# Eight consecutive w2 rows per partition, and the last outputs behind earlier DMAs

## The chip, the cores and the metric

The kernel runs on one core of one Trainium2 chip. The core has a tensor engine (PE), a vector engine (DVE), a scalar engine (ACT), GpSimd (POOL in the profile) and a sync engine (SP), which share an on-chip memory of 128 partitions. Sixteen DMA engines move data between it and the device memory. In this kernel GpSimd and SP issue the DMAs. The metric is the time of one execution on the device, in microseconds; the median of several runs counts.

## The reference

Two layers run one after the other. The first is attention over 8 batches, 8 heads, 576 positions and a head size of 64. Four heads look back over a window of 32 positions, the other four over every fourth position in a window of 128. The second is a soft mixture of 8 experts with 4 slots each:

```python
x = attn_out.transpose(0, 2, 1, 3).reshape(4608, 512)
logits = x @ phi                        # 4608 x 32
d = softmax(logits, axis=0)             # over the rows
slot_input = (d.T @ x).reshape(8, 4, 512)
for e in range(8):
    h = np.maximum(slot_input[e] @ w1[e], 0.0)   # 4 x 1024
    slot_out[e] = h @ w2[e]                      # w2[e]: 1024 x 512
c = softmax(logits, axis=1)
out = c @ slot_out.reshape(32, 512)     # 4608 x 512
```

All inputs and the output are fp32. The slots need every row of x, so nothing of the output can start before the attention of all batches, the weights w1 and w2 of the experts, and the small products between them are done.

## The kernel before

The kernel casts every input to fp16 while it is loaded: only GpSimd's DMAs (the calls on `nc.gpsimd`) do this here, so all loads stand in GpSimd's order. A loop over the batches runs in three slots each (`slot0`, `slot1`, `slot2`), which lay out by hand in which order scores, exponentials, products with v, and the products for the mixture are issued, two batches deep. The loads of later batches and of the weights are issued from inside these slots (`weights`, lines 531 to 563): w1 in the first six batches and at the start of the seventh, w2 from the seventh on. Before a GpSimd load is issued, the load issued eight places before must have landed.

**w2.** Each expert's w2 has 1024 rows of 512 numbers. `load_w2` (line 217) brings them into a tile of 128 partitions, 8 rows each. In the kernel before, partition p holds rows 4p to 4p+3 in its first half and rows 512+4p to 512+4p+3 in its second, so a partition is filled from two runs of 8 KB in the device memory. There are three forms of load:

- whole experts (1 to 5): one DMA of all 128 partitions (line 219);
- expert 0: one DMA of partitions 0 to 95, and later four DMAs of 8 partitions each (`load_w2_eight`, line 523: partitions 96+j, 100+j, ... 124+j). Each of these four is followed by a tiny load of 8 x 8 numbers into `turn`, which nothing reads;
- experts 6 and 7: four DMAs each (line 227), by column half and by rows 0 to 3 or 4 to 7 of each partition. The first column halves of both come first.

**From slots to h.** After the batches, PE computes h for all 32 slots in two PSUM tiles of 512 columns, `hps[0]` and `hps[1]` (line 686). ACT and DVE take half the columns of each with a relu into `h_sb[fc]` (lines 696 and 697). Four PE transposes per tile (line 699) pick every fourth column, to match the rows that a partition of w2 holds; copies on DVE and ACT put the result into `hTm` (line 703).

**The output.** `slot_out` (line 718) multiplies `hTm` by w2, one column half at a time, and ACT copies the result to `so_sb`. Then `out` is made in pairs of 128-row blocks. Rows of the first pairs 0 to 7 are made in two column halves (`combine`), those of pairs 8 to 17 whole (`combine_full`). A pair is a product on PE, a scaling out of PSUM on ACT or DVE, and an output DMA. The order of the last ones is: whole pair 13, half pair 3, whole 14, half 4, whole 15, half 5, half 6, half 7, whole 16, whole 17. All go out by GpSimd in fp16, cast on the way, except whole pairs 16 and 17: these are written in fp32 and go out by SP.

**The buffers at the end.** Pairs 16 and 17 use two fp32 buffers that are used once before: `last0` by whole pair 15, and `last1` by half pair 5 (in fp16, in a part of the buffer). So the scaling of pair 16 has to wait until the output DMA of whole pair 15 has landed, and that of pair 17 until that of half pair 5 has.

The lines that matter:

```python
in_=moe_w2[e].rearrange("(h p l) n -> p h (l n)", h=2, l=4)[rows],          # line 221
nc.tensor.transpose(hT[fc][:, c, :], h_sb[fc].rearrange("p (k l) -> p l k", l=4)[:, c, :], ident)   # 699
if (half, pair) == (1, 5):                                                   # 764, takes "last1"
tag = "last1" if pair == NFIN // 2 - 1 else "last0"                          # 794, NFIN // 2 is 18
```

Of the kernel before, what the change touches and what calls it, by code (L numbers as in the profile page):

```python
# [9 lines left out]
FP32 = mybir.dt.float32  # L10
FP16 = mybir.dt.float16
U32 = mybir.dt.uint32
AF = mybir.ActivationFunctionType
# [11 lines left out]
DMODEL = H * D  # L25
# [3 lines left out]
FDIM = 1024  # L29
# [12 lines left out]
NFIN = N_ROWS // 128  # L42
UNITS = 7
MASKED = -60000.0
NH = DMODEL // 2
# [4 lines left out]
def kernel(  # L50
# [10 lines left out]
    nc = tc.nc  # L61
# [11 lines left out]
    ident = consts.tile([128, 128], FP16, name="ident")  # L73
# [14 lines left out]
    w2t = {e: w2a_pool.tile([128, 8, DMODEL], FP16, name=f"w2_{e}", tag=f"w2_{e}") for e in range(2)}  # L88
# [12 lines left out]
    for i in range(NV):  # L101
        slab = fix.tile([128, V_SLAB], FP16, name=f"v{i}", tag=f"v{i}")
        n = NT * 4 * VW
# [113 lines left out]
    def load_w2(e, half=None, rows=slice(0, 128)):  # L217
        if half is None:
            nc.gpsimd.dma_start(  # L219
                out=w2t[e].rearrange("p (h l) n -> p h (l n)", h=2)[rows],  # L220
                in_=moe_w2[e].rearrange("(h p l) n -> p h (l n)", h=2, l=4)[rows],
            )
            return
        src = moe_w2[e].rearrange("(h p l) n -> h p l n", h=2, l=4)
        c0 = NH * half
        for h in range(2):
            nc.gpsimd.dma_start(
                out=w2t[e][:, 4 * h : 4 * h + 4, c0 : c0 + NH], in_=src[h][:, :, c0 : c0 + NH]
            )


# [291 lines left out]
    def load_w2_eight(j):  # L523
        load_w2(0, rows=slice(96 + j, 128, 4))
        nc.gpsimd.dma_start(out=turn[0:8, 8 * j : 8 * j + 8], in_=moe_w2[0, 0:8, 0:8])
# [131 lines left out]
    h_pool = tc.alloc_tile_pool(name="hp", bufs=1)  # L657
    out_pool = tc.alloc_tile_pool(name="outp", bufs=1)
# [5 lines left out]
    for g in range(4):  # L664
# [8 lines left out]
        out=diag,  # L673
# [6 lines left out]
    hps = [psum_e.tile([128, 512], FP32, name=f"hps{fc}", tag=f"hps{fc}") for fc in range(2)]  # L680
    for fc in range(2):
        for g in range(2):
            for dc in range(4):
                for j in range(4):
                    e = 4 * g + j
# [4 lines left out]
                        start=(g == 0 and dc == 0),  # L690
                        stop=(g == 1 and dc == 3),
                    )
    h_sb = [h_pool.tile([128, 512], FP16, name=f"h_sb{fc}", tag=f"h_sb{fc}") for fc in range(2)]
    hT = [psum_e.tile([128, 4, 128], FP16, name=f"hT{fc}", tag=f"hT{fc}") for fc in range(2)]
    for fc in range(2):
        nc.scalar.activation(out=h_sb[fc][:, 0:256], in_=hps[fc][:, 0:256], func=AF.Relu)
        nc.vector.tensor_relu(out=h_sb[fc][:, 256:512], in_=hps[fc][:, 256:512])
        for c in range(4):
            nc.tensor.transpose(hT[fc][:, c, :], h_sb[fc].rearrange("p (k l) -> p l k", l=4)[:, c, :], ident)
        hT4 = hT[fc].rearrange("p c (j s) -> p c j s", j=4)  # L700
        for g in range(2):
            dst = hTm[2 * g + fc].rearrange("p c (j s) -> p c j s", j=4)[:, :, :, 16 * g : 16 * g + 16]
            (nc.vector.tensor_copy, nc.scalar.copy)[g](out=dst, in_=hT4[:, :, :, 16 * g : 16 * g + 16])
# [30 lines left out]
    def combine_one(half, blk):  # L734
        fp = psum_f.tile([128, NH], FP32, name=f"f{half}_one{blk}", tag="f")
        cols = slice(NH * half, NH * half + NH)
        r0 = 128 * blk
        nc.tensor.matmul(fp, ET[:, r0 : r0 + 128], so_sb[:, cols], start=True, stop=True)
        ot = out_pool.tile([128, NH], FP16, name=f"oo{half}_{blk}", tag=f"oo{half}_{blk}")
        if blk % 2 == 0:  # L740
            nc.scalar.activation(out=ot, in_=fp, func=AF.Copy, scale=rrow[:, blk : blk + 1])
        else:
            nc.vector.tensor_scalar(
                out=ot, in0=fp, scalar1=rrow[:, blk : blk + 1], scalar2=None, op0=ALU.mult
            )
        nc.gpsimd.dma_start(out=out[r0 : r0 + 128, cols], in_=ot)

    def combine(half, pair):
        if half == 0 and pair == 0:
            combine_one(half, 0)  # L750
            combine_one(half, 1)
            return
        fp = psum_f.tile([128, 2, NH], FP32, name=f"f{half}_{pair}", tag="f")
        r0 = 256 * pair
        for k in range(2):
            nc.tensor.matmul(
                fp[:, k, :],
                ET[:, r0 + 128 * k : r0 + 128 * k + 128],
                so_sb[:, NH * half : NH * half + NH],
                start=True,  # L760
                stop=True,
                skip_group_check=True,
            )
        if (half, pair) == (1, 5):
            ot = out_pool.tile([128, 2, DMODEL], FP32, name="last1_a", tag="last1")
            ot = ot[:, 0, 0:NH].bitcast(FP16).rearrange("p (k n) -> p k n", k=2)
        else:
            ot = out_pool.tile(
                [128, 2, NH], FP16, name=f"ot{half}_{pair}", tag=f"ot{half}", bufs=NSPLIT // 2 - half
            )  # L770
        if pair % 2 == 0:
            for k in range(2):
                blk = 2 * pair + k
                nc.scalar.activation(
                    out=ot[:, k, :], in_=fp[:, k, :], func=AF.Copy, scale=rrow[:, blk : blk + 1]
                )
        else:
            nc.vector.tensor_tensor(
                out=ot,
                in0=fp,  # L780
                in1=rrow[:, 2 * pair : 2 * pair + 2, None].broadcast_to([128, 2, NH]),
                op=ALU.mult,
            )
        nc.gpsimd.dma_start(
            out=out[r0 : r0 + 256, NH * half : NH * half + NH].rearrange("(k p) n -> p k n", k=2),
            in_=ot,
        )

    def combine_full(pair):
        r0 = 256 * pair  # L790
        if pair < NFIN // 2 - 3:
            ot = out_pool.tile([128, 2, DMODEL], FP16, name=f"of_{pair}", tag="of", bufs=6)
        else:
            tag = "last1" if pair == NFIN // 2 - 1 else "last0"
            ot = out_pool.tile([128, 2, DMODEL], FP32, name=f"ol_{pair}", tag=tag)
            if pair == NFIN // 2 - 3:
                ot = ot[:, 0, :].bitcast(FP16).rearrange("p (k n) -> p k n", k=2)
        for k in range(2):
            blk = 2 * pair + k
            fp = psum_f.tile([128, DMODEL], FP32, name=f"f_{blk}", tag="f")  # L800
            nc.tensor.matmul(fp, ET[:, 128 * blk : 128 * blk + 128], so_sb, start=True, stop=True)
            if k == 0:
                nc.scalar.activation(
                    out=ot[:, k, :], in_=fp, func=AF.Copy, scale=rrow[:, blk : blk + 1]
                )
            else:
                nc.vector.tensor_scalar(
                    out=ot[:, k, :],
                    in0=fp,
                    scalar1=rrow[:, blk : blk + 1],  # L810
                    scalar2=None,
                    op0=ALU.mult,
                )
        (nc.gpsimd if pair < NFIN // 2 - 2 else nc.sync).dma_start(
            out=out[r0 : r0 + 256, :].rearrange("(k p) n -> p k n", k=2), in_=ot
        )

    with tc.manual_schedule(engines=None):
        slot_out(0, ORDER[:6])
        slot_out(1, ORDER[:6])  # L820
        slot_out(0, HALVED)
        at = {5: 0}
        for pair in range(NSPLIT // 2):
            combine(0, pair)
            if pair in at:
                slot_out(1, (HALVED[at[pair]],))
        slot_out(1, HALVED[1:])
        for pair in range(NSPLIT // 2, NFIN // 2 - 2):
            combine_full(pair)
            if pair >= NFIN // 2 - NSPLIT // 2:  # L830
                combine(1, pair - (NFIN // 2 - NSPLIT // 2))
        for pair in range(2):
            combine(1, NSPLIT // 2 - 2 + pair)
        for pair in range(2):
            combine_full(NFIN // 2 - 2 + pair)
# [36 lines left out]
```

The softmax here doesn't subtract the row's maximum and nothing guards it: scores larger than these inputs give would overflow.

## Time and profile before

| | |
|---|---|
| median of four runs | 183.19 us (182.41 to 183.41) |
| the profiled execution | 183.05 us, its span 181.4 us |
| PE / DVE / ACT / POOL busy | 81% / 59% / 50% / 46% of the span |
| DMA | 40.75 MB by written size, mean 225 GB/s |
| read / written in device memory | 61.93 MB / 9.44 MB |
| w2, whole experts (5 DMAs) | 1024 KB each, 19.4 us from issue to landing |
| w2, 96 partitions (1) | 768 KB, 18.0 us |
| w2, 8 partitions (4) | 64 KB each, 17.3 us |
| w2, halved (8) | 256 KB each, 9.8 us |
| the last two outputs, by SP | 512 KB each, 3.2 us |

The span runs from the first to the last instruction; the execution's own time has what lies around it too. The profile counts a loaded byte after the cast to fp16, so a rate in GB/s stands for twice as much read. "From issue to landing" includes the time that a DMA stands in the queue behind others. An engine's idle time costs nothing unless the engine is on the chain that ends last. In the views, "w" is any of the weight tiles, "of" and "ot" are output buffers of whole and half pairs, and "ol" is that of whole pairs 15 to 17.

### The profile page before, as it was taken

What the parts mean: (1) busy time and instruction counts of PE and PEld (TensorE: products, weight loads), DVE (VectorE), ACT (ScalarE), POOL (GpSimd) and SP (SyncE); (2) the same over time, 40 slices, a digit from 0 to 9 for tenths busy, and PEclk for the clock granted to TensorE, in tenths of its full rate; (3) what the DMA queues carried; (4) which work ended last, traced back from release to release, by engine and by line L of the source; (5) the groups of instructions that cost most, each with busy time, mean ns of one, the idle gap of its engine ahead of it and who ended that gap; (6) DMA issues with size and microseconds to landing.
All of it is one profiled execution on the core that took longest, in us unless ns stands there. A gap on an engine that the chain in (4) does not pass through costs nothing.

```text
span 181.4 us, 5591 instructions
## 1 busy us (share of the span) xinstructions
PE 146.4 (81%) x2464; PEld 87.6 (48%) x2464; DVE 107.3 (59%) x232; ACT 90.8 (50%) x162; POOL 83.7 (46%) x124
## 2 busy tenths in 40 slices
PE   0467977999999999999999999999987986588000
PEld 0134545746755665664674674674734363233000
DVE  4689785875757676588598498444504024388030
ACT  2044454748555484755765765766420115497020
POOL 7954473633624163261544346334410443989700
PEclk9999995798589789789999999999855699889855
DMA  4999999999999999999999999999999999999996
GB/s 62 195 192 209 205 212 215 201 212 213 202 212 214 202 211 216 201 214 209 204 213 211 204 215 215 213 213 211 215 216 211 200 194 172 333 360 410 407 342 231
DMA packets 29527, 40.75 MB, mean 225 GB/s; under 512 B 1856, under 2 KB 19264, under 8 KB 29504
## 3 DMA queue, kind: packets, MB, share of 16 engines
q0 software_dynamic: 28960, 39.36, 116.1%
q1 hardware_dynamic: 544, 1.05, 1.6%
q8 instruction: 19, 0.31, 0.6%
q14 instruction: 4, 0.03, 0.0%
HBM read 61.93 MB, written 9.44 MB: 394 GB/s over the span
## 4 chain that ended last, share of the span: by engine, by line
DMA 43%; PE 34%; ACT 6%; DVE 6%; POOL 5%; issue 3%; DVEq 0%; POOLq 0%
DMA w<-in_moe_w_dram 28%; DMA raw<-in_k_dram 9%; ACT p L293 5%; PE lg L408 5%; PE o_p L339 4%; PE sa L282 4%; DMA out_dram<-ol 4%; PE sb L271 4%; PE sa L271 4%; DMA out_dram<-ot 2%; PE rd L389 2%; DVE qk L245 2%; PE vb L163 2%; PE va L163 2%; PE u L452 2%
## 5 line engine op out<-in xcount | busy, mean ns | idle before, releaser
L293 ACT ACTIVATE p<-sa 128x960 f16<-128x960 f32 (+2 forms) x24 | 21.4, 890 | 34.0 <-PE sb L282 33.5
L339 PEld LDWEIGHTS <-p 128*128 128x128 f16 (+2 forms) x544 | 19.7, 99 | 12.8 <-issue 8.6
L245 DVE STREAM_TRANSPOSE qk<-raw 128x320 uint32<-128x320 uint32 (+1 forms) x32 | 21.5, 678 | 0.3
L271 PE MATMUL sa<-masks,ident 128*128 128x480 f16 (+2 forms) x48 | 15.6, 415 | 7.3 <-POOL masks L489 6.2
L293 ACT ACTIVATE p<-sb 128x960 f16<-128x960 f32 (+2 forms) x24 | 21.2, 885 | 0.0
L236 DVE STREAM_TRANSPOSE qk<-raw 128x576 uint32<-128x576 uint32 x16 | 19.8, 1248 | 1.7 <-DMA raw<-in_k_dram 1.2
L271 PEld LDWEIGHTS <-ident 128*128 128x128 f16 x96 | 9.6, 112 | 18.9 <-issue 7.7
L282 PEld LDWEIGHTS <-qk 32*128 32x128 f16 x832 | 12.7, 101 | 12.0 <-issue 9.8
L408 PE MATMUL lg<-xTd,phi 128*128 128x288 f16 x32 | 18.3, 659 | 0.0
L339 PE MATMUL o_p<-v,p 128*128 128x65 f16 (+1 forms) x288 | 16.6, 202 | 0.8 <-ACT v L172 0.7
L282 PE MATMUL sa<-qk 32*128 32x160 f16 (+4 forms) x416 | 16.6, 218 | 0.8 <-DVE qk L236 0.7
L282 PE MATMUL sb<-qk 32*128 32x160 f16 (+4 forms) x416 | 16.6, 218 | 0.0
L209 POOL COPY v<-v 32x1024 f16<-32x1024 f16 x8 | 8.3, 1033 | 17.4 <-PE sb L282 10.3
L271 PE MATMUL sb<-masks,ident 128*128 128x480 f16 (+2 forms) x48 | 15.5, 411 | 0.5 <-ACT p L293 0.5
L212 POOL DMA_DIRECT2D w<-in_moe_w_dram x16 | 8.9, 556 | 14.4 <-DMA vs<-in_v_dram 6.4
L361 DVE TENSOR_TENSOR xp<-o_p,rc_p 128x448 f16<-128x448 f32 (+1 forms) x24 | 14.5, 602 | 0.9
L361 DVE TENSOR_TENSOR xd<-o_d,rc_d 128x448 f16<-128x448 f32 (+1 forms) x24 | 14.5, 602 | 0.8
L219 POOL DMA_DIRECT2D w<-in_moe_w_dram x10 | 6.7, 671 | 14.5 <-DMA w<-in_moe_w_dram 8.1
L163 PE MATMUL va<-vs,orders 32*128 32x256 f16 (+1 forms) x96 | 12.1, 289 | 1.0 <-ACT p L293 1.0
L412 ACT ACTIVATE ET<-lg 128x288 f16<-128x288 f32 x16 | 6.6, 410 | 12.3 <-PE lg L408 12.1
L360 DVE RECIPROCAL rc_p<-o_p 128x7 f32<-128x7 f32 (+1 forms) x24 | 4.7, 196 | 11.8 <-PE o_p L339 11.3
L382 ACT COPY xTp<-rp 128x576 f16<-128x576 f16 x16 | 10.4, 648 | 2.2 <-PE rp L377 2.2
(108 smaller groups left out, 277.9 us busy)
## 6 DMA issues: line engine op xcount, KB each, us to landing
w<-in_moe_w_dram POOLq DMA_DIRECT2D x16, 512.0 KB, 16.3
w<-in_moe_w_dram POOLq DMA_DIRECT2D x5, 1024.0 KB, 19.4
vs<-in_v_dram POOLq DMA_DIRECT2D x8, 512.0 KB, 14.2
raw<-in_q_dram POOLq DMA_DIRECT2D x7, 576.0 KB, 16.6
raw<-in_k_dram POOLq DMA_DIRECT2D x7, 576.0 KB, 16.9
out_dram<-ot POOLq DMA_DIRECT2D x14, 256.0 KB, 4.1
out_dram<-of POOLq DMA_DIRECT2D x7, 512.0 KB, 4.9
w<-in_moe_w_dram POOLq DMA_DIRECT2D x8, 256.0 KB, 9.8
```

Of the source, the lines that this page charges most:

```text
L163: nc.tensor.matmul(o.rearrange("p (h d) -> p h d", h=4), l, st[:, 0:4, D * r : D * r + D], start=(r == 0), stop=(r == DIL - 1), skip_group ...
L209: nc.gpsimd.tensor_copy(out=vL[b % NV][0:32, :, :, 0:D], in_=vD[b % NV][96:128, :, :, 0:D])
L212: nc.gpsimd.dma_start(out=w1t[e][:, 2 * i : 2 * i + 2, :].rearrange("p l f -> p (l f)"), in_=moe_w1[e, 256 * i : 256 * i + 256].rearrange( ...
L236: nc.vector.transpose(out=dst, in_=src)
L245: nc.vector.transpose(out=o, in_=i)
L271: nc.tensor.matmul(sps[h // 2][:, h % 2, 0:n], ident, bias[g], start=True, stop=False, skip_group_check=True,)
L282: nc.tensor.matmul(sps[h // 2][:, h % 2, c0 : c0 + w], kt_[32 * h : 32 * h + 32, k0 : k0 + 128, tt], qt_[32 * h : 32 * h + 32, q0 : q0 + w ...
L293: nc.scalar.activation(out=pt, in_=sps[ab][:, :, 0:n], func=AF.Exp, scale=SCALE)
L339: nc.tensor.matmul(o[p0 : p0 + np_, n, :], l, rr, start=(k == 0), stop=(k == len(jobs) - 1), skip_group_check=True,)
L361: nc.vector.tensor_tensor(out=x.rearrange("p t (h d) -> p (t h) d", h=4)[0:nq, u0:u1, :], in0=o[0:nq, 0:n, 0:D], in1=rc[0:nq, 0:n, None].b ...
L382: nc.scalar.copy(out=xTp_t[b][:, c, :], in_=rg)
L408: nc.tensor.matmul(lp, phi4[:, kc].rearrange("p c s -> p (c s)"), rhs, start=(kc == 0), stop=(kc == 3))
```

## The change

Partition p of a w2 tile now holds rows 8p to 8p+7, one run of 16 KB in the device memory. Whole loads and the 8-partition loads have one run per partition in place of two. The halved loads keep their number and the size of their pieces, and take rows 0 to 3 or 4 to 7 of each partition. To match, the transposes pick every eighth column of h, so `h_sb` is one tile of 1024 columns, and both relu pairs stand ahead of all eight transposes. At the end, half pair 4 uses `last0` in place of half pair 5 using `last1`; whole pair 15 moves to `last1`. So pair 16 waits for the DMA of half pair 4, and pair 17 for that of whole pair 15.

```diff
             nc.gpsimd.dma_start(
-                out=w2t[e].rearrange("p (h l) n -> p h (l n)", h=2)[rows],
-                in_=moe_w2[e].rearrange("(h p l) n -> p h (l n)", h=2, l=4)[rows],
+                out=w2t[e].rearrange("p l n -> p (l n)")[rows],
+                in_=moe_w2[e].rearrange("(p l) n -> p (l n)", l=8)[rows],
             )
             return
-        src = moe_w2[e].rearrange("(h p l) n -> h p l n", h=2, l=4)
+        src = moe_w2[e].rearrange("(p l) n -> p l n", l=8)
         c0 = NH * half
         for h in range(2):
             nc.gpsimd.dma_start(
-                out=w2t[e][:, 4 * h : 4 * h + 4, c0 : c0 + NH], in_=src[h][:, :, c0 : c0 + NH]
+                out=w2t[e][:, 4 * h : 4 * h + 4, c0 : c0 + NH], in_=src[:, 4 * h : 4 * h + 4, c0 : c0 + NH]
             )
...
-    h_sb = [h_pool.tile([128, 512], FP16, name=f"h_sb{fc}", tag=f"h_sb{fc}") for fc in range(2)]
+    h_sb = h_pool.tile([128, FDIM], FP16, name="h_sb")
     hT = [psum_e.tile([128, 4, 128], FP16, name=f"hT{fc}", tag=f"hT{fc}") for fc in range(2)]
     for fc in range(2):
-        nc.scalar.activation(out=h_sb[fc][:, 0:256], in_=hps[fc][:, 0:256], func=AF.Relu)
-        nc.vector.tensor_relu(out=h_sb[fc][:, 256:512], in_=hps[fc][:, 256:512])
+        c0 = 512 * fc
+        nc.scalar.activation(out=h_sb[:, c0 : c0 + 256], in_=hps[fc][:, 0:256], func=AF.Relu)
+        nc.vector.tensor_relu(out=h_sb[:, c0 + 256 : c0 + 512], in_=hps[fc][:, 256:512])
+    for fc in range(2):
         for c in range(4):
-            nc.tensor.transpose(hT[fc][:, c, :], h_sb[fc].rearrange("p (k l) -> p l k", l=4)[:, c, :], ident)
+            nc.tensor.transpose(
+                hT[fc][:, c, :], h_sb.rearrange("p (k l) -> p l k", l=8)[:, 4 * fc + c, :], ident
+            )
...
-        if (half, pair) == (1, 5):
-            ot = out_pool.tile([128, 2, DMODEL], FP32, name="last1_a", tag="last1")
+        if (half, pair) == (1, 4):
+            ot = out_pool.tile([128, 2, DMODEL], FP32, name="last0_a", tag="last0")
...
-            tag = "last1" if pair == NFIN // 2 - 1 else "last0"
+            tag = "last0" if pair == NFIN // 2 - 2 else "last1"
```

## The prediction

> **What bounds the kernel now.** I read the page's slices first, then the chain of work that ended last, then windows over its last third, then the timeline there, and last the trace's records of single DMAs.
>
> The slices:
>
> ```profile
> DMA  4999999999999999999999999999999999999996
> GB/s 62 195 192 209 205 212 215 201 212 213 202 212 214 202 211 216 201 214 209 204 213 211 204 215 215 213 213 211 215 216 211 200 194 172 333 360 410 407 342 231
> ```
>
> The 16 DMA engines are busy from the second slice to the last but one. Loads are read as fp32 and written as fp16, so 213 GB/s written is 426 GB/s read. From slice 35 on they are writing the output. The chain says the same:
>
> ```profile
> 102.30 21.25 DMA w<-in_moe_w_dram
> ...
> 124.99 19.69 DMA w<-in_moe_w_dram
> ...
> 146.42 9.80 DMA w<-in_moe_w_dram
> 156.22 0.04 issue
> 156.26 0.32 PE so L722 x4
> ...
> 168.21 6.93 DMA out_dram<-ol
> 175.13 0.03 issue
> 175.16 0.05 DVEq L807
> 175.21 0.05 issue
> 175.26 0.47 DVE ol L807
> ```
>
> The reader is to see three terms: the weights arrive until 156.22; an output stage follows; then an eviction at 175.26 waits for an output DMA to land. The windows show the last two:
>
> ```profile
> 162.00:176.00 14.00, 4.91 (x23) 1.91 (x20) 5.63 (x10) 5.11 (x12) 9.07 (x13) 0.81 1.65 408
> 176.00:177.10 1.10, 0.00 (x0) 0.00 (x0) 0.67 (x2) 0.50 (x1) 0.00 (x0) 0.50 0.33 70
> 177.10:180.40 3.30, 0.00 (x0) 0.00 (x0) 0.00 (x0) 0.00 (x0) 0.00 (x0) 0.50 0.84 310
> ```
>
> The last columns are the DMA share and GB/s. The output runs at 408 GB/s until 176, then there is a hole of 1.1 us at 70 GB/s, and then the last 1 MB goes out. The timeline gives the reason for the hole and the slack of the stage before it:
>
> ```profile
> 146.62 3.21 PE L722 MATMUL so<-w,hTm 128*32 128x256 f16 x104 [0.38 <-DVE hTm L703]
> ...
> 150.88 0.29 PE L722 MATMUL so<-w,hTm 128*32 128x256 f16 x4 [1.05 <-DMA w<-in_moe_w_dram]
> ...
> 175.24 1.26 ACT L803 ACTIVATE ol<-f,rrow 128x512 f32<-128x512 f32 x2 [8.64 <-DMA out_dram<-ol]
> 175.26 1.41 DVE L807 TENSOR_SCALAR ol<-f,rrow 128x512 f32<-128x512 f32 x2 [8.28 <-DMA out_dram<-ol]
> 176.08 1.05 SPq L814 DMA_DIRECT2D out_dram<-ol  x2
> ```
>
> Both of SP's outputs are issued only at 176.08 and 176.75, because ACT and DVE sat idle for over 8 us until the buffers were free.
>
> [...] at each 8-partition load, eight engines need 0.63 us (two pieces) and the other eight about 0.2 us. [...] The trace puts it at 3.4 ns: one engine's share of a 1 MB load (16 pieces of 4 KB written) takes 4.89 us, of a 256 KB load (32 pieces of 512 B) 1.315 us; without an overhead the second would be a quarter of the first, 1.22, so 0.095 us goes to the 28 pieces that it has above a quarter of 16 (32 - 4). [...] No output of before runs beside another queue, but instruction fetches do run between the loads.
>
> **The outputs at the end.** Pair 16's eviction now waits for the DMA of pair 15 (issued 168.21, landed 175.13), pair 17's for that of combine(1, 5) (168.92, landed 175.68). After the change combine(1, 4) and pair 16 share last0; pair 15 and pair 17 share last1. So pair 16 waits for a DMA issued at 167.49, which lands at 173.74, and pair 17 for the one that lands at 175.13. From landing to SP's issue takes 0.95 us (175.13 to 176.08: ACT and DVE in parallel, 0.75 the longer), so SP issues at 173.74 + 0.95 = 174.69 and at 176.08, against 176.08 and 176.75. From issue to the first packet takes 0.93 us (176.08 to 177.01), so data starts at 175.62 and could start at 177.01. GpSimd's queue runs dry at about 176.2 (stragglers to 176.5); SP's 1 MB takes 177.01 to 179.85, that is 2.84. New end of data: at 175.62 there is still 0.6 us of GpSimd's data, then 2.84 of SP's, without a pause: 175.62 + 0.6 + 2.84 = 179.05, against 179.85. The second SP output is not late: the first keeps the engines until about 177.6. The gain is 0.8 us; the hole in the packets (176.2 to 177.0) is 0.8 too. The landing of pair 15 at 175.13 comes before any SP data, so what pair 17 waits for isn't slowed. On ACT and DVE nothing but pair 17 is behind the waiting eviction, on SP only its own second output; GpSimd's issues wait for none of these; the combine(1, 4) and pair 15 evictions are the first users of their buffers, as last1_a and pair 15 were. Bounds: no gain (0) if the two queues hinder each other as much as the hole costs; 0.95 if the stragglers at 176.2 to 176.5 are filled too.
>
> **The full w2 loads.** Six MB (five loads of 1 MB, and expert 0 in one of 96 partitions and four of 8) change from pieces of 4 KB written to pieces of 8 KB: per engine 96 pieces become 48. At 3.4 ns each that saves 0.16 us. No trace of before shows a piece of 16 KB read by GpSimd's queue. From one side, a cut back into 4 KB pieces gives 0; from the other, a worse pattern of HBM addresses [...] could slow each piece. The trace speaks against that: pieces of 1 KB, 4.6 KB and 8 KB read all lie on one line[...]. GpSimd's issue gets cheaper (0.72 us with 256 pieces, 0.56 in the w1 loads with 128), hidden, since it waits for landings of the eighth DMA before (8.1 and 10.7 us at lines 219 and 227). The halved loads (line 227) keep 512 pieces of 512 B at other addresses: 0.
>
> **The 8-partition loads.** The trace has 16 landings per DMA. Eight engines show a lag that matches the instruction fetches: 19 of 16 KB, about 0.95 us each, whose durations repeat with a period of eight. Hence the last load lands on its first engine at 152.22 and on its last at 156.22; this spread is what the end of the loads is made of. By the packets, the loads for j = 0 and 2 run on one half of the engines (call it X) and those for j = 1 and 3 on the other (Y), while all four `turn` DMAs, which have one run per partition, run on X. X holds six of the fast engines and two lagging ones, Y six lagging and two fast. At the end X's last engine lands at 155.22, Y's at 156.22. If one run per partition puts all four loads on X, X gets 2 x (0.63 - 0.2) = 0.86 more and Y 0.86 less: X ends at 156.08, Y at 155.36, and the end moves by 0.14. If they alternate as now: 0. If all go to Y: 156.22 + 0.86, a loss of 0.86. I take 0.07, between the first two, which I hold about equally likely.
>
> **The transposes.** h_sb becomes one tile, and each transpose takes columns 8 apart, so all eight need the evictions of both halves. Now hps is complete at 144.75, ACT's second eviction ends at 145.19, DVE's at 145.76 (it stands behind a copy of hT); the first transposes end at 145.1 and the first `so` matmul starts at 145.49, the long run at 146.62. After: ACT to 145.19, DVE to about 145.6, eight transposes from 145.65 (0.42 per four), the first pair of copies (DVE 0.29, ACT 0.37) from 146.1, the second from 146.5, so the last hTm is there at about 147.25 in place of 146.97, and the run of 104 ends 0.3 later, at 150.15. It is hidden by the wait of 1.05 us for w at 150.88, of which 0.75 remains. Without that cover it costs 0.3 once, on the first half's outputs alone; these leave GpSimd at 158.8, 0.57 before the second half's first output, so even then most is hidden. Copies, transposes and matmuls keep their number and shapes.
>
> **Sum.** The end of the loads comes 0.16 + 0.07 = 0.23 us earlier. It passes on one to one: `so` at 156.26, line 801 at 157.03, the first full output at 159.37, for which GpSimd has waited 0.57 us; behind it the 408 GB/s stretch shifts as a whole. With 0.8 at the end: 1.03 us. The profiled execution took 183.05 (span 181.4, some 1.7 around it), so 182.0; the median of the runs shown is 183.19, 0.14 above it, so I predict 183.19 - 1.03, rounded to 182.1.
>
> **Rivals.** *Only the end gains*: pieces of 8 KB cost what two of 4 KB do, the 8-partition loads alternate still. For it: `turn` and the loads follow no simple cursor in this trace. Time: 183.19 - 0.8 = 182.4. *The end gives nothing or the balance gets worse*: SP's data beside GpSimd's hinder each other, or all four 8-partition loads go to Y: 183.19 - 1.03 + 0.8 to 0.93 = 183.0 to 183.1. Against the second: the first of them should stay on X[...]. *Slower*: the 16 KB reads are slower per byte. Place: 115 to 145 us, 48 pieces per engine, now 2 x 304.5 = 609 ns for the same bytes. To be 0.5% slower the loads must lose 0.92 + 0.8 = 1.7 us, 36 ns a piece, 6%; from about 645 ns a piece it decides. At 10% it is 2.9 us: 183.19 - 0.8 + 2.9 = 185.3. For it: no such piece has been seen; against it: the straight line above. *More than forecast*: landings draw together by more than I count, 0.5 us further: 181.5.
>
> **How the numbers follow.** Forecast 0.48 (its own range 181.8 to 182.4), only the end 0.22, nothing at the end or worse balance 0.14, slower 0.10, more 0.06. Bound of a measurable difference: 0.5%, 0.92 us, so 182.27 and 184.11. Below 182.27 lie about 0.40 of the forecast's 0.48, 0.06 of the second and the 0.06 of the last: 0.52. Above 184.11: 0.10. Between: 0.38. The range from 181.4 to 183.3 leaves out the slower case and the edges.
>
> **What would show it.** SP's two output issues near 174.5 and 175.9 and no hole below 300 GB/s ahead of SP's data: the end is right. Two issues within 0.7 us of each other, or a hole as before, says it is wrong. Landings of full w2 loads 4.85 us apart or less on one engine and only half the packets: the pieces are right; 5.2 us would be the slower rival. The wait for w ahead of the last matmuls of the first half must stay above zero, about 0.7 us; if it turns into a wait for hTm, the transposes cost more than I say. The last w2 landing near 155.9 is the sum of both; later than 156.6 makes the forecast wrong whatever the end gains.

## The result and the profile after

The changed kernel has a median of 182.01 us over 35 executions (181.53 to 183.76), the kernel before 182.97 us over 56 (182.28 to 183.63). The ratio of the two is 0.9964, with a 95% interval of 0.9952 to 0.9976: 0.65 us faster, 0.44 to 0.88, which is inside the 0.5% that was called measurable. The medians lie further apart (0.96 us) than the ratio says, because the new times are not spread as the old ones are: 18 of the 35 lie between 181.53 and 182.01, and 17 from 182.22 on, most of them near 182.7. The median stands at the upper edge of the early group. The mean, 182.28, is 0.66 below that of before, 182.94. An execution more than 1.5% above the fastest of its kernel is left out of a ratio; in what follows this was one, of 185.11 us.

The profiled execution is one of the early group: 181.84 us, its span 180.1. These are its slices, to be held against those of before:

```profile
DMA  4999999999999999999999999999999999999995
GB/s 62 194 194 210 206 210 214 204 210 214 203 212 216 201 212 214 202 212 211 205 211 211 208 210 217 218 218 209 217 218 209 200 190 189 304 389 409 411 397 210
DMA packets 28727, 40.75 MB, mean 226 GB/s; under 512 B 1824, under 2 KB 19232, under 8 KB 27936
```

In the w2 stretch (the 25th to the 30th number) the rate is 217 or 218 GB/s in five of the six slices, where it was 213 to 216, and 209 in the other, where it was 211. There are 800 packets less (29527 before). The chain of work that ended last:

```profile
102.07 21.30 DMA w<-in_moe_w_dram
...
124.65 19.77 DMA w<-in_moe_w_dram
...
146.16 9.61 DMA w<-in_moe_w_dram
155.77 0.04 issue
155.82 0.32 PE so L726 x4
...
167.43 7.16 DMA out_dram<-ol
174.59 0.03 issue
174.62 0.05 DVEq L811
174.66 0.05 issue
174.71 0.75 DVE ol L811
```

The last w2 landing is at 155.77 (156.22 before), and what ends the chain is still a whole pair that waits for the output DMA of pair 15; but now it is pair 17. The timeline of the last outputs, and the windows (columns as before, the last two DMA share and GB/s):

```profile
173.43 0.69 ACT L807 ACTIVATE ol<-f,rrow 128x512 f32<-128x512 f32 x1 [8.19 <-DMA out_dram<-last_a]
173.47 0.75 DVE L811 TENSOR_SCALAR ol<-f,rrow 128x512 f32<-128x512 f32 x1 [7.86 <-DMA out_dram<-last_a]
174.29 1.63 SPq L818 DMA_DIRECT2D out_dram<-ol  x2
174.69 0.69 ACT L807 ACTIVATE ol<-f,rrow 128x512 f32<-128x512 f32 x1 [0.58 <-DMA out_dram<-ol]
174.71 0.75 DVE L811 TENSOR_SCALAR ol<-f,rrow 128x512 f32<-128x512 f32 x1 [0.49 <-DMA out_dram<-ol]
```

```profile
174.00:175.00 1.00, 0.00 (x0) 0.00 (x0) 0.51 (x2) 0.42 (x2) 0.00 (x0) 0.50 1.98 401
175.00:176.00 1.00, 0.00 (x0) 0.00 (x0) 0.46 (x1) 0.38 (x1) 0.00 (x0) 0.50 1.32 378
176.00:177.00 1.00, 0.00 (x0) 0.00 (x0) 0.00 (x0) 0.00 (x0) 0.00 (x0) 0.50 1.03 375
177.00:178.00 1.00, 0.00 (x0) 0.00 (x0) 0.00 (x0) 0.00 (x0) 0.00 (x0) 0.50 1.02 385
```

The two evictions are 1.25 us apart, each behind its own DMA, and no microsecond falls below 375 GB/s up to 178. The hole of 1.1 us at 70 GB/s is gone. So the end looks as forecast. If that is right, what is missing from 1.03 us lies in the loads, and the two groups of times are the lead.

### The profile page after: what moved, and what is told of

Read it like the earlier page. It is cut to its first block, busy times and chain, and to the rows that moved or that the text cites. A ratio compares the mean times of both kernels' runs of the same rounds, so it can differ in the third digit from the quotient of the medians.

```text
span 180.1 us, 5591 instructions
## 1 busy us (share of the span) xinstructions
PE 143.1 (79%) x2464; PEld 85.4 (47%) x2464; DVE 107.3 (60%) x232; ACT 90.3 (50%) x162; POOL 82.5 (46%) x124
## 4 chain that ended last, share of the span: by engine, by line
DMA 71%; DVE 7%; PE 6%; POOL 5%; issue 4%; ACT 3%; POOLq 0%; DVEq 0%
DMA w<-in_moe_w_dram 37%; DMA raw<-in_k_dram 11%; DMA raw<-in_q_dram 10%; DMA vs<-in_v_dram 9%; DMA out_dram<-ol 4%; DVE qk L245 2%; ACT of L807 1%; POOL raw L138 1%; DVE qk L236 1%; PE f L805 1%; PE o_p L339 1%; ACT ot L778 1%; DVE ol L811 1%; POOL w L227 1%; PE sa L282 1%
## 5 line engine op out<-in xcount | busy, mean ns | idle before, releaser
L212 POOL DMA_DIRECT2D w<-in_moe_w_dram x16 | 8.8, 553 | 25.7 <-DMA vs<-in_v_dram 12.2
L271 PE MATMUL sa<-masks,ident 128*128 128x480 f16 (+2 forms) x48 | 14.6, 390 | 7.3 <-POOL masks L489 6.2
L271 PEld LDWEIGHTS <-ident 128*128 128x128 f16 x96 | 9.1, 106 | 18.1 <-issue 7.2
L282 PEld LDWEIGHTS <-qk 32*128 32x128 f16 x832 | 12.1, 97 | 11.2 <-issue 9.0
L282 PE MATMUL sa<-qk 32*128 32x160 f16 (+4 forms) x416 | 16.0, 213 | 0.8 <-DVE qk L236 0.7
L282 PE MATMUL sb<-qk 32*128 32x160 f16 (+4 forms) x416 | 16.1, 214 | 0.0
L271 PE MATMUL sb<-masks,ident 128*128 128x480 f16 (+2 forms) x48 | 14.4, 387 | 0.2 <-ACT p L293 0.2
L219 POOL DMA_DIRECT2D w<-in_moe_w_dram x10 | 5.5, 549 | 17.1 <-DMA w<-in_moe_w_dram 10.4
L227 POOL DMA_DIRECT2D w<-in_moe_w_dram x8 | 6.0, 758 | 11.0 <-DMA w<-in_moe_w_dram 11.0
```

Source lines behind the costliest of these rows:

```text
L212: nc.gpsimd.dma_start(out=w1t[e][:, 2 * i : 2 * i + 2, :].rearrange("p l f -> p (l f)"), in_=moe_w1[e, 256 * i : 256 * i + 256].rearrange( ...
L271: nc.tensor.matmul(sps[h // 2][:, h % 2, 0:n], ident, bias[g], start=True, stop=False, skip_group_check=True,)
L282: nc.tensor.matmul(sps[h // 2][:, h % 2, c0 : c0 + w], kt_[32 * h : 32 * h + 32, k0 : k0 + 128, tt], qt_[32 * h : 32 * h + 32, q0 : q0 + w ...
```

## The experiments

**The end alone, and the w2 layout alone.** The first puts the new buffers into the kernel before:

```diff
-        if (half, pair) == (1, 5):
-            ot = out_pool.tile([128, 2, DMODEL], FP32, name="last1_a", tag="last1")
+        if (half, pair) == (1, 4):
+            ot = out_pool.tile([128, 2, DMODEL], FP32, name="last0_a", tag="last0")
...
-            tag = "last1" if pair == NFIN // 2 - 1 else "last0"
+            tag = "last0" if pair == NFIN // 2 - 2 else "last1"
```

> The kernel before with the new buffers of the last outputs alone. If the hole ahead of SP's data is what the tail costs: 0.8 us faster than before (ratio about 0.9956), SP's two issues near 174.7 and 176.1, no hole. If the two queues hinder each other: no change. If the w2 layout makes the two groups of times of the changed kernel (around 181.7 and 182.8), this one keeps a single spread of about 1.3 us, as before.

Measured: ratio 0.9955 (0.9943 to 0.9968), 0.82 us faster (0.59 to 1.04), 18 executions from 181.56 to 182.70 with no gap wider than 0.31 us. Its timeline has SP's issues where they were expected:

```profile
173.84 0.69 ACT L803 ACTIVATE ol<-f,rrow 128x512 f32<-128x512 f32 x1 [7.24 <-DMA out_dram<-last_a]
...
174.71 1.67 SPq L814 DMA_DIRECT2D out_dram<-ol  x2
175.15 0.69 ACT L803 ACTIVATE ol<-f,rrow 128x512 f32<-128x512 f32 x1 [0.62 <-DMA out_dram<-ol]
```

The second takes the same lines back in the changed kernel.

> The new w2 layout with the old buffers of the last outputs. By the forecast 0.2 us faster than before (ratio about 0.9987). If all four 8-partition loads on one half of the engines make the end of the loads depend on which engines get a third instruction fetch, the times fall into two groups about 0.9 us apart, the early one some 0.3 to 0.6 us faster than before, the late one some 0.3 us slower, and the mean near no change.

Measured: ratio 1.0002 (0.9980 to 1.0024): no gain, within 0.4 us either way. The 14 executions fall into two groups with nothing between them, nine from 182.25 to 182.62 and five from 183.39 to 184.06. The clock of the tensor engine doesn't tell them apart: 0.868 to 0.909 of full speed in the early group, 0.875 to 0.910 in the late one. So the end gives the gain, the layout gives none that the average shows, and the groups come with the layout.

**Expert 0 without the 8-partition loads.** In the changed kernel:

```diff
-                load_w2(0, rows=slice(0, 96))
+                load_w2(0)
...
-                load_w2_eight(0)
...
-                load_w2_eight(1)
...
-            load_w2_eight(2)
...
-            load_w2_eight(3)
```

> The changed kernel with expert 0 loaded by one DMA of 128 partitions, without the four 8-partition loads and the four tiny ones. If these loads balance the engines as counted (four on the half with six fast engines), the lagging half now ends later by about a quarter of 4 x 0.63 us spread evenly: every engine gets 2 more pieces of 8 KB in place of 4 or 0, so the half without them gains 1.2 us of work, the other loses 1.2; against that eight DMAs of 0.2 us each per engine go: about 0.3 us slower to 0.5 faster than the changed kernel, in one group of times. If the 8-partition loads don't matter: the same two groups as the changed kernel.

Measured: ratio 0.9938 (0.9913 to 0.9962), six executions from 181.28 to 182.07. The late times are gone. The expectation had the better side of its range right. But this version also has eight DMAs less, so it doesn't show by itself that the placement was the cost.

**Which engines small loads take.** The tiny loads get other sizes:

```diff
-        nc.gpsimd.dma_start(out=turn[0:8, 8 * j : 8 * j + 8], in_=moe_w2[0, 0:8, 0:8])
+        r = (6, 2, 4, 12)[j]
+        nc.gpsimd.dma_start(out=turn[0:r, 8 * j : 8 * j + 8], in_=moe_w2[0, 0:r, 0:8])
```

> The changed kernel with tiny loads of 6, 2, 4 and 12 partitions in place of 8 each, to see which engines a small load takes. If a small load always starts at the same engine, the engines with 16-byte packets are the first 6, 2 and 4 of those of the 8-partition loads, and the 8-partition loads stay on their half; if there is a cursor that goes on by the number of partitions, the 8-partition loads of j = 1, 2, 3 begin 6, 8 and 12 engines further on. Time as the changed kernel.

Measured: 182.85 us, a late time. The 16-byte packets tell the engines apart by how far each lags behind the first. The load of 2 partitions ran on engines with lags of 0 and 0.76 us, that of 4 on lags of 0, 0.37, 0.76 and 1.20, that of 6 on 0, 0.04, 0.39, 0.76, 1.22 and 2.51. Each set holds the smaller one, as it would if all of them started at one engine, and the 8-partition loads stayed on that side. The first four of these engines lag by 1.20 us at most; of the eight, two lag by more than 2 us. In the changed kernel's own trace the four tiny loads have the same pattern of lags (0, 0.03, 0.09, 0.39, 0.68, 1.19, 1.21 and 2.42 us at the first) but for one engine that falls back by 1.09 us, from 1.19 to 2.28, and the 8-partition loads are on the same half as the tiny ones: all four on one half, called X in the prediction.

**Two runs per partition for expert 0, in the new layout.** Its tile gets a gap between its halves, so that the 8-partition loads have two runs again, and the products with this expert read that tile; the other experts keep the new loads, and the number of DMAs stays:

```diff
+    w2pad = w2a_pool.tile([128, 2, 4 * DMODEL + 16], FP16, name="w2_0p", tag="w2_0p")
...
+        if e == 0:
+            nc.gpsimd.dma_start(
+                out=w2pad[rows, :, 0 : 4 * DMODEL],
+                in_=moe_w2[e].rearrange("(p h l) n -> p h (l n)", h=2, l=4)[rows],
+            )
+            return
...
```

> The changed kernel, but expert 0's tile has 16 unused elements between its halves, so that its loads take two runs per partition again, at 8 consecutive rows. Theory: the four 8-partition loads on one half of the engines, together with the instruction fetches [...], decide which engine ends the loads. With two runs they should go to both halves by turns as before, so each half gets two: the late group of times (182.6 and later in the changed kernel) goes away and the median is 181.9 or earlier, in one spread of about 1.2 us. Rival: the placement doesn't matter (the old layout of the other experts does); then the two groups stay, half and half, with the late one near 182.8.

Measured: ratio 0.9942 (0.9923 to 0.9962), six executions from 181.54 to 182.39, median 181.67. In its trace the loads for j = 1 and 3 run on the half that the tiny loads leave free, those for j = 0 and 2 on the same half as these, as in the kernel before. Against the changed kernel (0.9964, 0.9952 to 0.9976) the placement would be worth about 0.4 us, but the intervals overlap, so the times alone don't fix that size. The late group is gone in these six.

**The changed kernel once more**, unchanged, for its records:

> The changed kernel once more, to see its records at another position of the instruction fetches. If the third fetch falls on one of the two fetched engines among those of the 8-partition loads, the last w2 landing is near 156.8 and the time near 182.9; if not, near 155.8 and 181.8. If the fetches have nothing to do with the two groups, time and position are unrelated.

Measured: 182.83 us. The page counts 19 packets on the instruction queue in each of the two profiles. Their durations repeat with a period of eight (974, 974, 961, 893, 893, 948, 945, 936 ns), which fits one for each of eight engines, and the cycle starts elsewhere in the two profiles. Read so, 19 fetches give three of the eight engines a third one, not the same ones each time; the last of the three comes only at about 153 us (152.84 in the first profile). From the packets and the landings of four profiles of the new layout with all four loads on X, with the first two of the three:

```
                              third fetches (ns)   last w2 landing   time
changed kernel                948, 945             155.77            181.84
w2 layout alone               948, 945             155.85            182.60 (early group)
changed kernel, once more     961, 893             156.78            182.83
tiny loads of other sizes     961, 893             156.81            182.85
```

The link is seen directly, too. Of the eight engines of the tiny loads, the last stands 2.42 us behind the first at the third and at the fourth tiny load of the first profile, with a fetch of 945 ns between them at 140.25. In the second it goes from 2.29 to 3.38 between them, and the fetch of 893 ns starts at 140.96, between the two. That engine has two 8-partition loads more than before, and now a third fetch: it ends the loads. The same jump, 1.09 us on one engine of X, stands in the first profile and in those of the w2 layout alone, the end alone and the two runs per partition, each time with a fetch of 893 ns between the two tiny loads, and fetches of other durations leave these lags as they are. So the two fetched engines of X are those of 893 ns. They end the loads in the early profile as well, at 155.63 and 155.77 against 154.88 for the last of the others, but there neither has a third fetch. By the order of the durations, four of the eight positions of the cycle give one of them a third fetch: an estimate of one late execution in two, if all positions are equally frequent, beside the 17 of 35 above and the 5 of 14 with the w2 layout alone.

The chain of this execution has the landing 1.0 us later than the other:

```profile
147.18 9.61 DMA w<-in_moe_w_dram
156.78 0.04 issue
156.83 0.43 PE so L726 x4
```

**The old pieces without 8-partition loads.** The kernel before with the new end and expert 0 in one DMA, against the same in the new layout:

```diff
-                load_w2(0, rows=slice(0, 96))
+                load_w2(0)
```

> The old w2 layout and transposes, the new buffers of the last outputs, expert 0 by one DMA, no 8-partition and no tiny loads. Beside the run with one DMA in the new layout it isolates the pieces of 4 KB against 8 KB. By the landings of the profiles (4.89 against 4.83 us per MB on one engine) six loads of 1 MB take 0.33 us more with the old pieces: ratio to before about 0.9956 against 0.9938. If the pieces don't matter, the same as in the new layout; if the two relus ahead of all transposes cost something, this is the faster one.

Measured: ratio 0.9955 (0.9939 to 0.9971), against 0.9938 (0.9913 to 0.9962) with pieces of 8 KB. The difference of 0.31 us is near the expected 0.33, but the intervals overlap, so the times don't show it, and the landings show less. In these two traces seven engines get no fetch between the first and the sixth full load; on them the 5 MB take 24.31 to 24.35 us in the new layout and 24.46 to 24.52 in the old one, which is 0.03 us per MB. The 4.83 us of the expectation (130.25 to 135.08 in the changed kernel) is one engine alone: the eight that get no fetch there take 4.81 to 4.87, those of the kernel before 4.87 to 4.91. And 0.9955 is also the ratio of the end alone: with the old pieces, spread by turns, the 8-partition loads were worth nothing that these times show.

**The cost doubled, which it wasn't.**

```diff
-                load_w2(0, rows=slice(0, 96))
+                load_w2(0, rows=slice(0, 64))
...
-        load_w2(0, rows=slice(96 + j, 128, 4))
-        nc.gpsimd.dma_start(out=turn[0:8, 8 * j : 8 * j + 8], in_=moe_w2[0, 0:8, 0:8])
+        load_w2(0, rows=slice(64 + 2 * j, 128, 8))
+        load_w2(0, rows=slice(65 + 2 * j, 128, 8))
```

> The changed kernel with the suspected cost doubled: expert 0 by one DMA of 64 partitions and eight of 8 partitions (a second 8-partition load in place of each tiny one, so the number of DMAs is the same). The half of the engines that takes the small loads gets 12 pieces of 8 KB for expert 0 in place of 10, the other 4 in place of 6. Theory: two fetched engines are in the loaded half; they now end the loads in every execution, 2 x 0.6 = 1.2 us later than in the changed kernel for each position of the fetches: two groups again, near 183.0 and 184.1, ratio to before 1.003 or more. Rival, that the placement of these loads doesn't matter: as the changed kernel, ratio 0.9964.

Measured: ratio 0.9950 (0.9932 to 0.9968), nine executions from 181.42 to 182.31. The expectation failed, because its premise did: in the landings of the trace every engine has a piece in exactly one load of each pair, so the two loads of a pair go to different halves. Every engine then has 8 pieces for expert 0, as with one DMA, and the time is near that run's. It says nothing against the placement, but it was not the test that it was meant to be. So the uneven share was raised in the form in which the changed kernel has it:

```diff
-                load_w2(0, rows=slice(0, 96))
+                load_w2(0, rows=slice(0, 80))
...
-        load_w2(0, rows=slice(96 + j, 128, 4))
+        load_w2(0, rows=slice(80 + j, 128, 6))
...
                 load_w2_eight(1)
+                load_w2_eight(4)
...
             load_w2_eight(3)
+            load_w2_eight(5)
```

> The changed kernel with six 8-partition loads, each followed by its tiny load, and a DMA of 80 partitions for expert 0. In the changed kernel all four such pairs went to the same half of the engines, while pairs of two 8-partition loads (the doubled run) went to both halves by turns, so this raises the uneven share that the doubled run didn't raise: 11 pieces of 8 KB against 5, in place of 10 against 6, with four DMAs more. Theory: the fetched engines of the loaded half end the loads 0.6 + 0.2 us later, so the times go up by about that: ratio to before near 1.000 to 1.002, late times of 183.5 and more. Rival, that placement is not what separates the changed kernel from the runs at 0.994 and 0.995: ratio near 0.9964 plus 0.001 for the four DMAs. If the loads go to both halves, no late group and near 0.995.

Measured: ratio 1.0029 (1.0010 to 1.0047), 19 executions from 182.34 to 184.35, eleven of them above 183.3, and the one of 185.11 us that is left out. That is 1.2 us slower than the changed kernel, somewhat more than the 0.7 to 1.0 expected. All tiny and 8-partition loads were on one half in its trace. The trace has a second effect, too: GpSimd waited 4.5 us until 146.01 for a load to land on its last engine, and the rate fell to 123 GB/s in the 33rd of its 40 slices, because most of the other engines had run out of loads. The last engine had not; its landings follow each other every 1.32 to 1.43 us from 148.24 to 155.02.

The effect of the placement can be told from that of the fetches. Six profiles have the cycle of fetches at the same position (third fetches of 961 and 893 ns before the end of the loads):

```
                              8-partition loads        last w2 landing
old pieces, one DMA           none                     156.04
the end alone (old layout)    two on each half         156.11
eight of them, no tiny loads  four on each half        156.29
changed kernel, once more     four on X                156.78
tiny loads of other sizes     four on X                156.81
six of them                   six on X                 157.69
```

More on that half ends the loads later, less ends them earlier.

**A better use of the small loads.** In the run with one DMA for expert 0:

```diff
+    def load_w2_four(j):
+        load_w2(0, rows=slice(112 + j, 128, 4))
...
-                load_w2(0)
+                load_w2(0, rows=slice(0, 112))
...
```

with one such load after the loads of experts 1, 4, 3 and 5 each.

> No 8-partition loads: expert 0 by one DMA of 112 partitions and four of 4 partitions, without the tiny ones. The run with tiny loads of 2 and 4 partitions showed that small loads start at the same engine each time and that the first four of these engines get no instruction fetches. If the lag of the fetched engines ends the loads, taking one 8 KB piece of 0.6 us from them and adding four short DMAs [...] makes the loads end 0.3 to 0.4 us earlier than with one DMA for expert 0: 181.3 or a ratio to before near 0.992. If the balance doesn't matter: as with one DMA, 0.9938.

Measured: ratio 0.9921 (0.9906 to 0.9937), six executions from 181.19 to 181.62, the lowest ratio here and the narrowest spread. Its chain:

```profile
145.81 9.66 DMA w<-in_moe_w_dram
155.47 0.04 issue
155.52 0.32 PE so L724 x4
```

For expert 0, one DMA gives each engine 8 pieces of 8 KB. Here 112 partitions give 7, and if the four loads of 4 partitions took the engines that the tiny one of 4 took in the run with other sizes (lags of 1.20 us at most), these four engines have 11. The run beats the kernel before by 1.45 us and the changed one by about 0.8. Against the run with one DMA (0.9938) the intervals overlap, but the two profiles have their fetches at the same position of the cycle, and the last landing is at 155.47 here and at 156.12 there.

## Why the prediction was right in range and wrong in a step

The forecast was 182.1 us, from a gain of 1.03 us: 0.8 at the end, 0.16 from larger pieces, 0.07 from the placement, nothing from the transposes. The measured gain, 0.44 to 0.88 us, leaves 1.03 out. That the median of 182.01 lies so near to 182.1 is in part luck. The forecast started from 183.19, the median of four executions, 0.22 above that of 56; the new median stands at the upper edge of its early group; and 183.19 - 1.03 is 182.16, which rounds to 182.2.

*The end* was right, in mechanism and size: 0.82 us with the new buffers alone against 0.8. There SP's issues came at 174.71 and 176.00, forecast for 174.69 and 176.08, and the data ended at 179.03, forecast for 179.05. In the changed kernel, where 0.23 was to be taken off, the issues start at 174.29 and after 175.4, the rest of the difference being the earlier loads of that execution. The hole is gone, and the rival that the two queues hinder each other is out.

*The larger pieces* were right in mechanism and about right in size. The landings give 0.03 us per MB on an engine, that is 4 ns for each of the 8 pieces saved where 3.4 was counted, and about 0.2 us in all beside the forecast 0.16. The 3.4 ns are an estimate from two sizes (4.89 us for 1 MB, 1.315 for 256 KB); from the same two follow 2.45 us for a w1 load of 512 KB and 2.77 for a q or k load of 576 KB, and on the engine that lands first the trace of before has 2.43 to 2.47 and 2.76 to 2.80. The rival that reads of 16 KB are slower per byte, which needed 5.2 us per MB, is out: on engines without a fetch 1 MB takes 4.81 to 4.87.

*The placement of the 8-partition loads* is the step that failed. The prediction had where they would go right (all four on X) and had seen that X holds two lagging engines. But it took the end of each half from one execution, 155.22 for X and 156.22 for Y, as if these were fixed, and so counted 0.86 us more on X as a gain of 0.14, or 0.07 in the mean with no change. That execution had its third fetches of 974 and 974 ns before the end of the loads, so neither fetched engine of X had one. Where this holds in the new layout, too, the loads end where the prediction's sum put them: 155.77 and 155.85, near its 155.9. Where one of the two gets a third fetch, the end is 156.78 and 156.81, an engine's setback of 1.09 us later, and past the 156.6 that the prediction itself named as the sign that it was wrong. The price should have been a mean over the positions of the fetches. By the run with two runs per partition it was a loss of about 0.4 us, an estimate that the times alone don't fix; at equal positions of the cycle, the landings with an even placement are earlier by 0.23 us (155.54 against 155.77) and 0.49 us (156.29 against 156.78). Summed: 0.82 + 0.2 - 0.4 = 0.6, against the 0.65 measured (0.44 to 0.88). The rival *only the end gains*, a gain of 0.8, described the sum of the parts better than the forecast did, though not for its reason: the layout gained on its own and lost it again through the placement.

*The transposes* were hidden as forecast. They now run behind all four evictions:

```profile
140.62 0.71 PE L701 MATMUL hT<-ident,h_sb 128*128 128x128 f16 x8 [0.95 <-DVE h_sb L698]
...
150.46 0.29 PE L726 MATMUL so<-w,hTm 128*32 128x256 f16 x4 [1.03 <-DMA w<-in_moe_w_dram]
```

The wait for w before the first half's last matmuls is 1.03 us, so the cover is there; 0.7 had been expected. That execution reached h some four microseconds earlier than the profile of before, so the cover was more than the code alone gives. The profile with two runs per partition reached h as late as before, and there the cover was used up: the matmuls start at 146.76 (146.62 before) and show no wait for w until the first half is done. It cost nothing that the end shows, since the second half still waited 1.09 us for its last w and the execution took 181.56 us.

What kept the gain below the forecast is therefore one term, mis-sized and wrong in sign: a balance among DMA engines, read from one execution, of something that changes with each.

## What to carry to other kernels

The loads followed each other without a pause here, and in the changed kernel's profile the last of them landed on its first engine at 151.63 us and on its last at 155.77: what ended them was the last engine, not the mean. In such a case a share moved between engines has to be priced against every position of what disturbs them, and separate groups in the times of one kernel are a reason to ask for such a cause. A saving per piece is to be read from several engines: one engine alone gave 0.06 us per MB here, seven gave 0.03. A buffer chosen so that its last user waits for a DMA one step earlier was worth the hole that it closed, and the hole could be read in advance from issue, landing and first packet. When an experiment is meant to raise a cost, check in its trace that the cost was raised before its time is read.

## What was not expected of the hardware

Small loads with one run per partition stayed on one side wherever an 8-partition load was followed by a tiny one: the tiny loads of 2, 4 and 6 partitions on engines that hold those of the smaller ones (lags of 0 and 0.76 us in all three), the 8-partition loads on the same half, four of four in the changed kernel and six of six where there were six. Two 8-partition loads of one run in succession went to different halves, in all four pairs of the doubled run; and with two runs per partition those for j = 1 and 3 changed their half though a tiny load stood between. A cursor that goes on by the number of partitions, which the expectation of the run with other sizes named as a possibility, fits the second of these alone; what decides the side was not settled.

The instruction fetches were 19 packets of 16 KB in each of the two profiles of the changed kernel, of 0.89 to 0.98 us in the first, and their durations repeat with a period of eight. That eight of the sixteen engines carry them is read from this period and from the lags. A fetch of 893 ns between two tiny loads went with a setback of 1.09 us on one engine of X, in the five profiles named above.
